# Routing one-hots and token products from 2-byte operands, the chunk index innermost

## The chip, the cores and the metric

The kernel runs on one core of one Trainium2 chip. Times are device microseconds (us) from the start to the end of one execution; the numbers compared are medians of several executions.

## What is computed

Linear attention without a softmax, followed by a mixture of experts with one expert per token.

```python
kv  = einsum('bhsd,bhse->bhde', k, v)            # b=8, h=8, s=576, d=e=64
out = einsum('bhsd,bhde->bhse', q, kv)
x   = out / sqrt(mean(out**2, -1) + 1e-6) * g_norm   # heads joined: x is [4608, 512]
logits = x @ w_gate                              # [4608, 8]
e = argmax(logits, axis=1); gate = softmax(logits)[e]
# in order of the tokens: the n-th token of an expert gets slot n, up to capacity 1152
out[i] = gate[i] * (relu(x[i] @ w1[e]) @ w2[e])  # w1: 512 x 1024, w2: 1024 x 512; zero if not kept
```

## The kernel before

**Two stages.** The first stage takes the eight images one after another: k, v and q are loaded, TensorE forms k'v (L736), transposes q (L802) and multiplies (L820); ScalarE and VectorE copy the results out of PSUM into `o_sb`; squares are summed (L846, L851). Then comes the routing of the image, `route`, mostly small VectorE instructions: reciprocal roots by Newton steps (L896 to L903), logits, the expert `mv_all`, and the token's place `pos_all` among the tokens of its expert, for which TensorE counts over the 128 partitions (L971). A token's row goes to `x_dram`. An image has 576 tokens; they lie on 128 partitions in C = 5 chunks.

Meanwhile the weights of the expert with the most tokens so far are loaded and split into two 2-byte halves (`w1h`, `w1l`, `w2h`, `w2l`: L390 or L392 for the high half, L396 for the low half, L356 and L360 for their scale), and once five images are routed the first 384 tokens of that expert are gathered (L452), normalised (L460), transposed through one PSUM bank (L470), split (L700 and L478) and multiplied with its weights (L555, L560, L563, then L601).

The second stage goes through the eight experts by rank: 640 slots and fewer each, weights loaded and split for the next expert while TensorE multiplies for this one.

**The table.** What the second stage needs is a table of the tokens: for each expert and each slot the token's number. It is built by TensorE, in `enter` (L1016), one matmul per chunk and five per image, all adding up in one PSUM bank `tab`. The stationary operand `ohl` is a one-hot of the low seven bits of a token's place, 128 columns; the moving operand `rhs` has 96 columns: 48 pairs of expert and high bits of the place, for each the token's number in a high and a low part. `rhs` is the product of the column one-hot `ohh` (48 columns) with the two parts `tok_hl`. The one-hots compare an index with a constant row: `iota128` (L210) and `cols` (L247), filled by GpSimd at the start. The three instructions are `low_hot` (L998), `col_hot` (L1003) and `tokens` (L1009). `read_table` (L1102 on) turns the table into row numbers; it runs after image 4 for the early expert and after image 7 for all, and `rank_experts` puts the experts in order after that.

**Widths.** `ohl` and `rhs` are 2 bytes wide (float16), `ohh`, `cols`, `lo`, `col`, `tok_hl` 4 bytes (float32). The five chunks are the outermost index of `ohl`, `ohh` and `rhs` behind the partition.

**The order.** Every operation of both stages is entered in a `Plan` with its engine, or a choice of engines, and a planned duration in us; the plan works out start times by taking, engine by engine, the operation that can start first and by its key among equals, and the instructions are emitted in that order. Each engine takes its own instructions in the order in which they were emitted. In the line `o2 = V(0.73, low_hot, [lo], takes=(lh,))` 0.73 us is the planned duration on VectorE, `[lo]` what it waits for, and `lh` the buffer that it takes, which has one copy (`rings`). `TOKENS` gives `tokens` a choice: VectorE for 0.57 us or GpSimd for 2.0.

Of the kernel before, what the change touches and what calls it, by code (L numbers as in the profile page):

```python
# [10 lines left out]
F16 = mybir.dt.float16  # L11
F32 = mybir.dt.float32
I32 = mybir.dt.int32
AF = mybir.ActivationFunctionType
ALU = mybir.AluOpType
# [5 lines left out]
NHI = 6  # L21
# [19 lines left out]
LAG_ELSE = 0.21  # L41
SQUARES = 'XXAAX'
TOPS = ('VVVV', 'AAAA')
TOKENS = (('V', 0.57), ('P', 2.0))
FIRST = -50.0
KEY = 10.0
EARLY_TILES = 1
# [111 lines left out]
def attention_moe_kernel(  # L159
# [12 lines left out]
    nc = tc.nc  # L172
    NB, H, S, D = q.shape
    N, DM = out.shape
    E = w_gate.shape[1]
    F = w1.shape[2]
    P = 128
    C = 5
# [6 lines left out]
    NT = NB * C  # L185
    W = E * NHI

    cst = ctx.enter_context(tc.tile_pool(name="cst", bufs=1))
# [20 lines left out]
    iota128 = cst.tile([P, P], F32, name="iota128")  # L209
# [15 lines left out]
    nc.vector.tensor_scalar(out=tok1, in0=tok_i[:, 0], scalar1=pair[:, 1:2], scalar2=None, op0=ALU.add)  # L225
    nc.vector.tensor_copy(tok_i[:, 0], tok1)

    tok_hl = cst.tile([P, 2, NT], F32, name="tok_hl")
    nc.vector.tensor_scalar(out=tok_i[:, 1], in0=tok_i[:, 0], scalar1=63, scalar2=None, op0=ALU.bitwise_and)
    nc.vector.tensor_copy(tok_hl[:, 1], tok_i[:, 1])  # L230
    nc.vector.tensor_scalar(out=tok_i[:, 1], in0=tok_i[:, 0], scalar1=6, scalar2=None, op0=ALU.logical_shift_right)
# [11 lines left out]

    slot_pos = cst.tile([P, W], F32, name="slot_pos")
    nc.gpsimd.iota(slot_pos, [[0, E], [P, NHI]], base=0, channel_multiplier=1, allow_small_or_imprecise_dtypes=True)
    cols = cst.tile([P, W], F32, name="cols")
    nc.gpsimd.iota(cols, [[-64, E], [1, NHI]], base=64 * E, channel_multiplier=0, allow_small_or_imprecise_dtypes=True)  # L247
    desc8 = cst.tile([P, E], F32, name="desc8")
    nc.vector.tensor_scalar(out=desc8, in0=iota_e, scalar1=-1.0, scalar2=float(E), op0=ALU.mult, op1=ALU.add)

# [44 lines left out]
    mv_all = cst.tile([P, NT], F32, name="mv_all")  # L295
# [382 lines left out]
    tab, misc = bank("tab"), bank("misc")  # L678
# [13 lines left out]
    op = plan.op  # L692
# [163 lines left out]
    def bc(ap, n):  # L856
        return ap.rearrange("p (c o) -> p c o", o=1).broadcast_to([P, C, n])
# [3 lines left out]
    def route(b, oh, ssh, outs, sums):  # L861

        key = (b + 1) * C - SOON
        cs = slice(b * C, (b + 1) * C)
        o_sb, ss = oh.t, ssh.t.rearrange("p c h -> p (c h)")
        z = {}
        tile_ = lambda nm, shape, dt=F32, bufs=2: z.setdefault(nm, at.tile([P] + shape, dt, name=nm, bufs=bufs))
        ne = NEWTON[b]
        eng = {"V": nc.vector, "P": nc.gpsimd}
        fast = {"V": 0.11, "P": 0.32}[ne]  # L870
        V = lambda t, f, deps, **kw: op(("V", t), lambda e: f(), deps, key, **kw)
# [15 lines left out]
        o = V(0.1, half, sums + lasts.get(b - 2, []), takes=(), uses=(ssh,))  # L887
        o = V(0.1, guess, [o])
        o = V(0.1, guess2, [o])
# [18 lines left out]
        for i in range(3):  # L908
            for j in range(4):
                o = op((ne, fast), newton(i, j), [o], key)  # L910
        rinv = o
        lth, hh, rh, lh = new("lt"), new("ohh"), new("rhs"), new("ohl")
# [21 lines left out]
        o = V(0.65, logits, [lt], uses=(lth,))  # L934
        o = V(0.11, most, [o])
# [21 lines left out]
        o = V(0.11, firsts, [dl])  # L957
        o = V(0.11, which, [o])
# [24 lines left out]
        def position():  # L983
            nc.vector.tensor_reduce(out=pos_all[:, cs], in_=z["inc"], axis=AX.X, op=ALU.max)

        o = V(0.11, mine, [bp])
        reads.append(o)
        pos = V(0.11, position, [o])
        lo_i = V(0.07, lambda: nc.vector.tensor_scalar(out=tile_("lo_i", [C], I32), in0=pos_all[:, cs], scalar1=P - 1,
                                                       scalar2=None, op0=ALU.bitwise_and), [pos])  # L990
        hi_i = V(0.07, lambda: nc.vector.tensor_scalar(out=tile_("hi_i", [C], I32), in0=pos_all[:, cs], scalar1=7,
                                                       scalar2=None, op0=ALU.logical_shift_right), [pos])
        lo = V(0.07, lambda: nc.vector.tensor_copy(tile_("lo", [C]), z["lo_i"]), [lo_i])
        col = V(0.07, lambda: nc.vector.scalar_tensor_tensor(out=tile_("col", [C]), in0=mv_all[:, cs], scalar=64.0,
                                                             in1=z["hi_i"], op0=ALU.mult, op1=ALU.add), [hi_i])

        def low_hot():
            nc.vector.tensor_tensor(out=tile_("ohl", [C, P], F16, 1),  # L998
                                    in0=iota128.rearrange("p (o w) -> p o w", o=1).broadcast_to([P, C, P]),
                                    in1=bc(z["lo"], P), op=ALU.is_equal)  # L1000

        def col_hot():
            nc.vector.tensor_tensor(out=tile_("ohh", [C, W], F32, 1),  # L1003
                                    in0=cols.rearrange("p (o w) -> p o w", o=1).broadcast_to([P, C, W]),
                                    in1=bc(z["col"], W), op=ALU.is_equal)

        def tokens(e):
            s4 = [P, C, 2, W]
            eng[e].tensor_tensor(out=tile_("rhs", [C, 2, W], F16, 1),  # L1009
                                    in0=z["ohh"].rearrange("p c (o w) -> p c o w", o=1).broadcast_to(s4),  # L1010
                                    in1=tok_hl[:, :, cs].rearrange("p i (c o) -> p c i o", o=1).broadcast_to(s4),
                                    op=ALU.mult)

        def enter(e):
            for c in range(C):
                nc.tensor.matmul(tab[:, 0:2 * W], lhsT=z["ohl"][:, c, :], rhs=z["rhs"][:, c], start=(b == 0 and c == 0),  # L1016
                                 stop=(b == NB - 1 and c == C - 1), skip_group_check=True)

        o = V(0.32, col_hot, [col], takes=(hh,))
        o = op(TOKENS, tokens, [o], key, (rh,), (hh,))  # L1020
        o2 = V(0.73, low_hot, [lo], takes=(lh,))
        ent = op(("T", 0.21), enter, [o, o2] + enters[-1:] + readers.pop("tab", []), FIRST, (), (rh, lh))
        enters.append(ent)

# [7 lines left out]
        o = V(0.11, sums_, [ex])  # L1032
        o = V(0.07, plus, [o])
# [484 lines left out]
    op = plan.op  # L1518
# [200 lines left out]
```

## Time and profile before

| what | value |
|---|---|
| median of 3 runs | 569.44 us (569.03 to 570.95) |
| profiled execution | 574.34 us, its span 572.5 us |
| TensorE matmul busy | 530.4 us, 93% of the span |
| VectorE busy | 389.3 us, 68% |
| ScalarE busy | 256.6 us, 45% |
| GpSimd busy | 204.9 us, 36% |
| mean granted TensorE clock | 0.975 of full speed |

The span reaches from the first to the last instruction of the profiled execution. Busy shares are averages over stages that have different limits; the groups of rows further down are cut by stage and by instruction. In them PE is TensorE's matmul, PEld its weight load, DVE VectorE, ACT ScalarE, POOL GpSimd, SP the engine that issues loads.

### The profile page before, as it was taken

How to read it: one execution, taken by the hardware profiler on the slowest of the kernel's cores; microseconds unless marked ns; L12 is line 12 of the kernel's file. 1: busy time of each engine (PE TensorE's matmuls, PEld its weight loads, DVE VectorE, ACT ScalarE, POOL GpSimd, SP SyncE). 2: the span in 40 equal slices, each digit the busy share in tenths (PEclk: the TensorE clock that was granted, in tenths of full speed). 3: DMA queues.
4: the chain of work that ended last, by engine and by line, in shares of the span. 5: the costliest groups of instructions: out<-in, count | busy, mean ns of one | idle time of the engine just before them, and what ended most of it. 6: DMA issues, size and time to landing. Idle time of an engine off the chain costs nothing.

```text
span 572.5 us, 11807 instructions
## 1 busy us (share of the span) xinstructions
PE 530.4 (93%) x4450; PEld 365.0 (64%) x4450; DVE 389.3 (68%) x1064; ACT 256.6 (45%) x502; POOL 204.9 (36%) x246
## 2 busy tenths in 40 slices
PE   5999896886897999999999999999999999999995
PEld 4888785774544666546754675677477558648743
DVE  4488687799977989998998677295848606203800
ACT  1687675496412662644715525263353426212211
POOL 3003334354334373345506440742453374021011
PEclk9999898697999999999999999999999999999998
DMA  8999999543249789599678755563645233010000
GB/s 279 358 354 315 370 357 374 198 148 154 94 142 363 153 214 294 138 316 163 201 183 207 177 150 155 166 170 99 200 155 128 87 103 58 6 55 21 2 37 32
DMA packets 81905, 102.71 MB, mean 179 GB/s; under 512 B 39148, under 2 KB 63724, under 8 KB 80818
## 3 DMA queue, kind: packets, MB, share of 16 engines
q1 hardware_dynamic: 74240, 70.50, 43.3%
q0 software_dynamic: 7584, 31.38, 16.2%
q8 instruction: 37, 0.61, 0.4%
q14 instruction: 26, 0.21, 0.1%
q10 hardware_dynamic: 18, 0.02, 0.0%
HBM read 73.20 MB, written 20.68 MB: 164 GB/s over the span
## 4 chain that ended last, share of the span: by engine, by line
issue 32%; PE 31%; POOL 12%; DVE 12%; DMA 9%; ACT 2%; SPq 2%; POOLq 0%; DVEq 0%
PE hp L555 10%; PE yp L601 8%; POOL out_dram L631 4%; PE op L820 4%; POOL pair L488 4%; DMA q_sb<-in_q_dram 3%; DMA xs<-pair 3%; PE a L736 3%; POOL xg L452 2%; DVE w1l L396 2%; PE op L555 2%; POOL xm L460 2%; DVE ss L851 2%; PE qp L802 2%; DMA v_sb<-in_v_dram 1%
## 5 line engine op out<-in xcount | busy, mean ns | idle before, releaser
L555 PE MATMUL hp<-xs,w1h 128*128 128x320 f16 (+6 forms) x960 | 134.2, 292 | 1.9 <-DVE hl L563 0.9
L555 PEld LDWEIGHTS <-w1h 128*128 128x128 f16 x1024 | 99.6, 98 | 38.8 <-issue 6.3
L631 POOL DMA_INDIRECT out_dram<-ysb,si x42 | 42.7, 1016 | 161.3 <-ACT ysb L626 152.0
L601 PEld LDWEIGHTS <-hh 128*128 128x128 f16 x560 | 54.2, 98 | 63.2 <-issue 1.1
L560 ACT ACTIVATE hh<-hp 128x320 f16<-128x320 f32 (+7 forms) x64 | 41.0, 640 | 106.6 <-PE hp L555 101.9
L356 DVE TENSOR_REDUCE am<-raw 128x1 f32<-128x512 f32 x120 | 75.9, 674 | 6.6 <-DMA raw<-in_moe_w_dram 6.6
L626 ACT ACTIVATE ysb<-yp,ysc 128x512 f32<-128x512 f32 (+5 forms) x41 | 28.1, 685 | 99.9 <-PE yp L601 90.7
L555 PE MATMUL hp<-xs,w1l 128*128 128x320 f16 (+6 forms) x480 | 72.0, 292 | 0.0
L563 DVE SCALAR_TENSOR_TENSOR hl<-hp,hh 128x320 f16<-128x320 f32 (+7 forms) x64 | 47.4, 740 | 32.9 <-ACT hh L560 31.4
L601 PE MATMUL yp<-w2h,hh 128*128 128x512 f16 x272 | 65.3, 379 | 0.8 <-ACT ysb L626 0.8
L601 PE MATMUL yp<-w2l,hh 128*128 128x512 f16 x272 | 64.5, 379 | 0.0
L601 PE MATMUL yp<-w2h,hl 128*128 128x512 f16 x272 | 64.4, 379 | 0.0
L820 PE MATMUL op<-kv_bd,qt 128*128 128x144 f32 x320 | 55.6, 311 | 5.7 <-ACT o_sb L700 2.9
L555 PEld LDWEIGHTS <-w1l 128*128 128x128 f16 x512 | 49.9, 98 | 16.4
L452 POOL DMA_INDIRECT xg<-x_dram,gi x42 | 44.7, 1064 | 30.8 <-DVE gt L465 10.7
L616 DVE COPY yt<-yp 128x256 f32<-128x256 f32 (+4 forms) x7 | 2.9, 415 | 75.9 <-PE yp L610 66.3
L396 DVE SCALAR_TENSOR_TENSOR w2l<-raw,sw,w2h 128x512 f16<-128x512 f32 x64 | 50.1, 826 | 4.1 <-ACT w2h L390 4.1
L820 PEld LDWEIGHTS op<-kv_bd,qt 128*128 128x128 f32 x320 | 46.1, 203 | 9.5 <-ACT o_sb L700 5.0
L396 DVE SCALAR_TENSOR_TENSOR w1l<-raw,sg,w1h 128x512 f16<-128x512 f32 x64 | 50.6, 823 | 1.5 <-ACT w1h L390 1.5
L488 POOL TENSOR_TENSOR pair<-xm,pair 128x512 f16<-128x512 f32 (+5 forms) x26 | 33.7, 1295 | 49.7 <-ACT pair L484 49.6
L601 PEld LDWEIGHTS <-hl 128*128 128x128 f16 x280 | 27.2, 98 | 31.8
L460 POOL TENSOR_TENSOR xm<-xg 128x512 f32<-128x512 f32 (+5 forms) x34 | 39.8, 1170 | 16.2 <-DVE pair L488 11.1
(249 smaller groups left out, 708.5 us busy)
## 6 DMA issues: line engine op xcount, KB each, us to landing
raw<-in_moe_w_dram SPq DMA_DIRECT2D x64, 512.0 KB, 5.2
x_dram<-o_sb POOLq DMA_DIRECT2D x8, 720.0 KB
k_sb<-in_k_dram SPq DMA_DIRECT2D x16, 320.0 KB, 6.1
v_sb<-in_v_dram SPq DMA_DIRECT2D x16, 320.0 KB, 6.5
q_sb<-in_q_dram SPq DMA_DIRECT2D x16, 320.0 KB, 6.6
x_dram<-o_sb POOLq DMA_DIRECT2D x8, 576.0 KB
k_sb<-in_k_dram SPq DMA_DIRECT2D x16, 256.0 KB, 3.4
v_sb<-in_v_dram SPq DMA_DIRECT2D x16, 256.0 KB
```

The source lines that it names most:

```text
L356: nc.vector.tensor_reduce(out=am()[:, p:p + 1], in_=raw[:, sl(p)], axis=AX.X, op=ALU.max, apply_absolute_value=True)
L396: nc.vector.scalar_tensor_tensor(out=wl[:, sl(p)], in0=raw[:, sl(p)], scalar=z["s"], in1=wh[:, sl(p)], op0=ALU.mult, op1=ALU.subtract)
L452: nc.gpsimd.indirect_dma_start(out=self.xg[i][0:n], out_offset=None, in_=x_dram[0:self.rows, :], in_offset=bass.IndirectOffsetOnAxis(ap=se ...
L460: eng.tensor_tensor(out=self.xm[i][0:n].rearrange("p (h d) -> p h d", h=H), in0=xg[:, :, 0:D], in1=xg[:, :, D:D + 1].broadcast_to([n, H, D ...
L488: eng.tensor_tensor(out=pair[0:n, 1], in0=self.xm[i][0:n], in1=pair[0:n, 0], op=ALU.subtract)
L555: nc.tensor.matmul(self.view(hp)[:, v], lhsT=w[:, c, f * P:(f + 1) * P], rhs=x[:, c, u * hw:(u + 1) * hw], start=(t == 0 and c == 0), stop ...
L560: nc.scalar.activation(self.out(self.hh, j), self.view(hp), AF.Relu)
L563: nc.vector.scalar_tensor_tensor(out=self.out(self.hl, j), in0=self.view(hp), scalar=0.0, in1=self.out(self.hh, j), op0=ALU.max, op1=ALU.s ...
L601: nc.tensor.matmul(yp[0:n, 0:DM], lhsT=h[:, j, o:o + n], rhs=w[:, j, :], start=(m == 0), stop=(m == len(self.terms) - 1))
L626: nc.scalar.activation(self.ysb[0:n], yp[0:n, 0:DM], AF.Copy, scale=self.ysc[0:n, i:i + 1])
L631: nc.gpsimd.indirect_dma_start(out=(disjoint.pop() if disjoint else out)[:, :], out_offset=bass.IndirectOffsetOnAxis(ap=self.sidx[0:n, col ...
L820: nc.tensor.matmul(ph.t[:, p * 2 * XW:(p + 1) * 2 * XW], lhsT=qt.t[:, (2 * w + p) * P:(2 * w + p + 1) * P], rhs=x, start=True, stop=True)
```

## The change

The constants and the small index tensors become 2 bytes wide, `cols` is repeated for each chunk, a constant `lows` of 128 x 5 takes the place of `iota128` in the low one-hot, and the chunk index becomes the innermost one of `ohl`, `ohh` and `rhs`. In the two comparisons and in the product every operand then walks in steps of one element along the five chunks, and the matmul reads both its operands with a step of five elements (10 bytes). The planned durations are changed, and the token product loses its choice of GpSimd.

```diff
-TOKENS = (('V', 0.57), ('P', 2.0))
+TOKENS = ('V', 0.31)
...
-    tok_hl = cst.tile([P, 2, NT], F32, name="tok_hl")
+    tok_hl = cst.tile([P, 2, NT], F16, name="tok_hl")
...
-    cols = cst.tile([P, W], F32, name="cols")
-    nc.gpsimd.iota(cols, [[-64, E], [1, NHI]], base=64 * E, ...)
+    cols = cst.tile([P, W, C], F16, name="cols")
+    nc.gpsimd.iota(cols, [[-64, E], [1, NHI], [0, C]], base=64 * E, ...)
+    lows = cst.tile([P, P, C], F16, name="lows")
+    nc.gpsimd.iota(lows, [[1, P], [0, C]], base=0, ...)
...
-        lo = V(0.07, lambda: nc.vector.tensor_copy(tile_("lo", [C]), z["lo_i"]), [lo_i])
-        col = V(0.07, lambda: nc.vector.scalar_tensor_tensor(out=tile_("col", [C]), ...
+        lo = V(0.07, lambda: nc.vector.tensor_copy(tile_("lo", [C], F16), z["lo_i"]), [lo_i])
+        col = V(0.07, lambda: nc.vector.scalar_tensor_tensor(out=tile_("col", [C], F16), ...
...
         def low_hot():
-            nc.vector.tensor_tensor(out=tile_("ohl", [C, P], F16, 1),
-                                    in0=iota128.rearrange("p (o w) -> p o w", o=1).broadcast_to([P, C, P]),
-                                    in1=bc(z["lo"], P), op=ALU.is_equal)
+            nc.vector.tensor_tensor(out=tile_("ohl", [P, C], F16, 1), in0=lows,
+                                    in1=z["lo"].rearrange("p (o c) -> p o c", o=1).broadcast_to([P, P, C]), op=ALU.is_equal)
         def col_hot():
-            nc.vector.tensor_tensor(out=tile_("ohh", [C, W], F32, 1),
-                                    in0=cols.rearrange("p (o w) -> p o w", o=1).broadcast_to([P, C, W]),
-                                    in1=bc(z["col"], W), op=ALU.is_equal)
+            nc.vector.tensor_tensor(out=tile_("ohh", [W, C], F16, 1), in0=cols,
+                                    in1=z["col"].rearrange("p (o c) -> p o c", o=1).broadcast_to([P, W, C]), op=ALU.is_equal)
         def tokens(e):
-            s4 = [P, C, 2, W]
-            eng[e].tensor_tensor(out=tile_("rhs", [C, 2, W], F16, 1),
-                                    in0=z["ohh"].rearrange("p c (o w) -> p c o w", o=1).broadcast_to(s4),
-                                    in1=tok_hl[:, :, cs].rearrange("p i (c o) -> p c i o", o=1).broadcast_to(s4),
-                                    op=ALU.mult)
+            s4 = [P, 2, W, C]
+            eng[e].tensor_tensor(out=tile_("rhs", [2, W, C], F16, 1),
+                                 in0=z["ohh"].rearrange("p (o w) c -> p o w c", o=1).broadcast_to(s4),
+                                 in1=tok_hl[:, :, cs].rearrange("p i (o c) -> p i o c", o=1).broadcast_to(s4), op=ALU.mult)
         def enter(e):
             for c in range(C):
-                nc.tensor.matmul(tab[:, 0:2 * W], lhsT=z["ohl"][:, c, :], rhs=z["rhs"][:, c], ...
+                nc.tensor.matmul(tab[:, 0:2 * W], lhsT=z["ohl"][:, :, c], rhs=z["rhs"][:, :, :, c], ...
...
-        o = V(0.32, col_hot, [col], takes=(hh,))
+        o = V(0.18, col_hot, [col], takes=(hh,))
         o = op(TOKENS, tokens, [o], key, (rh,), (hh,))
-        o2 = V(0.73, low_hot, [lo], takes=(lh,))
+        o2 = V(0.4, low_hot, [lo], takes=(lh,))
```

## Rows read from the trace of the kernel before

**Rows 1.** Windows of 10 us: busy us (instructions), TensorE clock, DMA share, GB/s.
```profile
core 0: us, PE busy (x) PEld busy (x) DVE busy (x) ACT busy (x) POOL busy (x), PEclk, DMA share, GB/s
30.00:40.00 10.00, 9.62 (x129) 8.91 (x127) 9.33 (x40) 7.61 (x21) 0.00 (x0) 1.00 1.08 356
110.00:120.00 10.00, 9.55 (x74) 8.58 (x75) 8.94 (x26) 8.10 (x23) 9.05 (x7) 0.79 0.26 69
120.00:130.00 10.00, 6.52 (x48) 5.56 (x46) 9.94 (x22) 7.68 (x20) 3.12 (x3) 1.00 0.54 178
130.00:140.00 10.00, 5.82 (x37) 4.84 (x38) 9.88 (x38) 8.79 (x25) 6.79 (x15) 0.73 0.48 187
140.00:150.00 10.00, 9.27 (x60) 5.27 (x59) 9.05 (x42) 5.14 (x10) 4.33 (x4) 0.92 0.33 132
170.00:180.00 10.00, 7.57 (x41) 4.00 (x40) 5.31 (x20) 2.79 (x5) 4.40 (x5) 1.00 0.93 306
190.00:200.00 10.00, 10.00 (x60) 5.68 (x59) 9.80 (x29) 7.82 (x15) 4.57 (x5) 1.00 0.80 136
```

**Rows 2.** Groups of VectorE instructions, 28 to 180 us: busy us, mean ns | idle before.
```profile
L998 DVE TENSOR_TENSOR ohl<-iota,lo 128x640 f16<-128x640 f32 x8 | 6.7, 834 | 0.0
L1009 DVE TENSOR_TENSOR rhs<-ohh,tok_hl 128x480 f16<-128x480 f32 x7 | 4.5, 649 | 0.1
L702 DVE COPY kv_bd<-kvs 64x256 f32<-64x256 f32 x12 | 3.6, 300 | 2.9 <-ACT kvs L700 2.7
L1003 DVE TENSOR_TENSOR ohh<-cols,col 128x240 f32<-128x240 f32 x8 | 3.3, 414 | 0.0
L702 DVE COPY kvt<-a 128x256 f32<-128x256 f32 x2 | 0.8, 422 | 0.5 <-PE a L760 0.5
```

**Rows 3.** Time line, image 4: start us, us [idle before <-releaser].
```profile
107.50 0.64 DVE L1009 TENSOR_TENSOR rhs<-ohh,tok_hl 128x480 f16<-128x480 f32 x1
109.39 0.72 ACT L390 ACTIVATE w1h<-raw,sg 128x512 f16<-128x512 f32 x1 [5.18 <-DVE sg L385]
```

**Rows 4.** Time line, image 5, up to the first product of the early expert.
```profile
136.46 0.65 DVE L1009 TENSOR_TENSOR rhs<-ohh,tok_hl 128x480 f16<-128x480 f32 x1
...
137.03 0.68 DVE L478 TENSOR_TENSOR xs<-x,xs 128x512 f16<-128x512 f32 x1
...
137.85 0.88 PE L470 MATMUL x<-ident,xm 128*128 128x128 f32 x4 [0.32 <-DVE xs L478]
...
138.81 0.58 ACT L700 CAST xs<-x 128x512 f16<-128x512 f32 x1
...
139.44 1.44 PE L555 MATMUL op<-xs,w1h 128*128 128x384 f16 x4 [0.70 <-ACT xs L700]
```

**Rows 5.** Time line, image 6.
```profile
150.51 0.54 DVE L563 SCALAR_TENSOR_TENSOR hl<-op,hh 128x384 f16<-128x384 f32 x1
...
151.10 0.81 PE L555 MATMUL op<-xs,w1h 128*128 128x384 f16 x4 [0.88 <-DVE hl L563]
```

**Rows 6.** Time line, image 7, and the end of the chain behind it.
```profile
162.85 0.66 DVE L1009 TENSOR_TENSOR rhs<-ohh,tok_hl 128x480 f16<-128x480 f32 x1
...
163.70 0.38 PE L1016 MATMUL tab<-rhs,ohl 128*128 128x96 f16 x5
...
179.26 0.46 PE L470 MATMUL xp<-ident,xm 64*128 64x64 f32 x4 [2.16 <-DVE xm L460]
```

**Rows 7.** Instructions on `ohl`: ns min/median/max, first and last start us.
```profile
L1016 PEld LDWEIGHTS <-ohl x40: 95/98/151, 43.7 to 163.8; 128*128 128x128 f16 x40
L1016 PE MATMUL tab<-rhs,ohl x40: 203/206/288, 44.4 to 163.9; 128*128 128x96 f16 x40
L998 DVE TENSOR_TENSOR ohl<-iota,lo x8: 807/824/908, 42.0 to 161.7; 128x640 f16<-128x640 f32 x8
```

**Rows 8.** Line 283, the transposes of the gate weights, in the same columns.
```profile
L283 PEld LDWEIGHTS misc<-ident,wrow x8: 180/198/198, 3.8 to 4.6; 4*128 4x128 f32 x8
```

**Rows 9.** The page's costliest groups: busy us, mean ns of one.
```profile
L820 PEld LDWEIGHTS op<-kv_bd,qt 128*128 128x128 f32 x320 | 46.1, 203 | 9.5 <-ACT o_sb L700 5.0
```

**Rows 10.** Time line of the start: GpSimd's fills and the first use.
```profile
3.11 0.32 POOL L247 IOTA cols<- 128x48 f32 x1
3.32 2.10 POOL L681 MEMSET kv_bd<- 128x1152 f32 x2
...
13.87 0.82 ACT L700 COPY kv_bd<-kvs 64x256 f32<-64x256 f32 x2
```

More of the change, by code (lines that the diff above doesn't have):

```diff
@@ L245, in attention_moe_kernel @@
     nc.gpsimd.iota(slot_pos, [[0, E], [P, NHI]], base=0, channel_multiplier=1, allow_small_or_imprecise_dtypes=True)
-    cols = cst.tile([P, W], F32, name="cols")
-    nc.gpsimd.iota(cols, [[-64, E], [1, NHI]], base=64 * E, channel_multiplier=0, allow_small_or_imprecise_dtypes=True)
+    cols = cst.tile([P, W, C], F16, name="cols")
+    nc.gpsimd.iota(cols, [[-64, E], [1, NHI], [0, C]], base=64 * E, channel_multiplier=0, allow_small_or_imprecise_dtypes=True)
+    lows = cst.tile([P, P, C], F16, name="lows")
+    nc.gpsimd.iota(lows, [[1, P], [0, C]], base=0, channel_multiplier=0, allow_small_or_imprecise_dtypes=True)
     desc8 = cst.tile([P, E], F32, name="desc8")
@@ L992, in route @@
                                                        scalar2=None, op0=ALU.logical_shift_right), [pos])
-        lo = V(0.07, lambda: nc.vector.tensor_copy(tile_("lo", [C]), z["lo_i"]), [lo_i])
-        col = V(0.07, lambda: nc.vector.scalar_tensor_tensor(out=tile_("col", [C]), in0=mv_all[:, cs], scalar=64.0,
+        lo = V(0.07, lambda: nc.vector.tensor_copy(tile_("lo", [C], F16), z["lo_i"]), [lo_i])
+        col = V(0.07, lambda: nc.vector.scalar_tensor_tensor(out=tile_("col", [C], F16), in0=mv_all[:, cs], scalar=64.0,
@@ L1014, in enter @@
         def enter(e):
             for c in range(C):
-                nc.tensor.matmul(tab[:, 0:2 * W], lhsT=z["ohl"][:, c, :], rhs=z["rhs"][:, c], start=(b == 0 and c == 0),
+                nc.tensor.matmul(tab[:, 0:2 * W], lhsT=z["ohl"][:, :, c], rhs=z["rhs"][:, :, :, c], start=(b == 0 and c == 0),
                                  stop=(b == NB - 1 and c == C - 1), skip_group_check=True)
-        o = V(0.32, col_hot, [col], takes=(hh,))
+        o = V(0.18, col_hot, [col], takes=(hh,))
         o = op(TOKENS, tokens, [o], key, (rh,), (hh,))
-        o2 = V(0.73, low_hot, [lo], takes=(lh,))
+        o2 = V(0.4, low_hot, [lo], takes=(lh,))
```

## The prediction

> **What bounds the kernel now.** I read the windows first, to cut the span into stages, then the groups of VectorE instructions between 28 and 180 us, then the time lines around each place where the edited instructions run. The windows show three stages [rows 1]. Up to about 110 us the DMA share is at 1.0 and the loads set the pace: VectorE is 93% busy at 30 to 40 us, but so is TensorE, and the transfers cannot come sooner. From 110 to about 140 us the DMA share falls to 0.26 to 0.54, TensorE is down to 6.5 and 5.8 busy us of 10, and VectorE stands at 8.9 to 9.9 of 10: here the order of VectorE's queue sets the pace. From 140 to 180 us TensorE is mostly busy with the early expert but still loses 0.7 us in one window and 2.4 in another. From 190 us TensorE has 10.0 of 10, with VectorE close behind at 9.8; whatever is gained must be gained before that, and it comes through only if VectorE's work for the next expert is moved ahead along with TensorE's.
>
> **The three VectorE instructions.** Each image has one low one-hot (640 elements per partition), one column one-hot (240) and one token product (480). They take 834, 414 and 649 ns [rows 2], 1897 ns in all; one of the eight token products runs on GpSimd. From the first two, (834 - 414) / 400 elements is 1.05 ns an element, over 162 ns that do not depend on the length. The change makes all operands 2 bytes wide and puts the chunks innermost, so that every operand walks in steps of one element, in runs of five. No row shows a two-input VectorE instruction of that kind and of any length, so I bound it. At one end the element cost stays: nothing is saved. At the other it halves: 162 + 336, 162 + 126 and 162 + 244 ns, that is 498, 288 and 406, together 1192 ns and 0.71 us less per image. The nearest row for a halving is a copy of 256 4-byte elements inside SBUF, 300 ns against 422 ns for a copy of the same length out of PSUM [rows 2]: less 162 ns it is 0.54 against 1.02 ns an element, so this engine does halve its element cost where operands allow. I take the halving, and keep zero for the range.
>
> The runs are of five, an odd number. If two elements could not be paired across the end of a run, five elements would take three steps in place of five, the saving would be four fifths (0.57 us per image), and the sum below 1.8 us in place of 2.2.
>
> [...]
>
> **Where that saving is on the path.** Eight images times 0.71 is 5.7 us of VectorE time, but the eight low one-hots start between 42.0 and 161.7 us [rows 7], and five of them before 110 us. Image by image:
>
> Images 0 to 3: nothing, the loads hide them (the first window of [rows 1]); without that cover they would be worth 2.8 us.
>
> Image 4, at 106 to 108 us: the scale of the first expert weights stands behind its token product, and ScalarE starts splitting them at 109.39, having idled 5.18 us for that scale [rows 3]. But the last queries are still landing and TensorE is 9.55 busy in the next window, so I count half: 0.35 us.
>
> Image 5, at 135 to 137 us: the clearest place. Behind the token product of 136.46 stands the low half of the second group of gathered rows (137.03); that frees the one PSUM bank for the third transpose (137.85), whose cast (138.81) lets TensorE begin the early expert at 139.44 [rows 4]. All 0.71 us pass.
>
> Image 6, at 149 to 151 us: the low half of a hidden tile at 150.51 stands behind both one-hots, and TensorE idles 0.88 us for it [rows 5]. The two one-hots shrink by 0.46 us, and the wait with them.
>
> Image 7, at 161.7 us on: token product, table, slots and gathered rows follow one another, and TensorE idles 2.16 us at the end of that chain for the last group of rows [rows 6]. 0.71 us pass; the ranking of the experts and with it the loads of the next weights hang on the same VectorE queue, so they move ahead too.
>
> Sum: 0.35 + 0.71 + 0.46 + 0.71 = 2.2 us.
>
> **What is added.** The table matmul now reads both operands with a step of 10 bytes. The rows to hold against it are 98 ns for a contiguous 2-byte weight load and 206 ns for its matmul [rows 7], and 198 ns for a 4-byte load from four partitions with a step of 32 bytes [rows 8], no more than the 203 ns that the contiguous 4-byte loads take in the same trace [rows 9]. A strided stationary operand is not dearer there, so I take zero; the upper bound is that a load doubles to the 4-byte price, five times 105 ns, and that a 96-column matmul, five in 0.38 us [rows 6], doubles too: about 0.9 us per image, of which images 6 and 7 would feel 1.8 us and the others little.
>
> [...]
>
> GpSimd fills two larger constants at the start, 240 and 640 elements in place of 48. The 48 took 0.32 us [rows 10], 6.7 ns an element, so 880 elements take at most 5.9 us and the fill of the two zeroed matrices ends at about 11 us instead of 5.4. They are first written at 13.87 us, and GpSimd has nothing else to do before the first output writes: zero, hidden by 2.8 us even at that price. The token product that ran on GpSimd costs VectorE 0.4 us in an image that the loads hide. The casts that feed the new operands keep their length and only change the output type.
>
> **The order.** The emission order is worked out from planned durations, and those fall by 0.73 us per image. All later choices (ScalarE or VectorE, VectorE or GpSimd, which ready operation first) may fall differently, in both stages. The trace cannot price this; the waits of TensorE between 100 and 200 us are each at most 2.2 us [rows 6], and one or two such waits more or fewer is what I allow.
>
> **Rivals.** (a) The forecast, 2.2 us: chance 0.52. (b) The saving is absorbed. For it: between 140 and 180 us TensorE is itself busy for most of the time, and behind a shorter VectorE queue it may wait for gathered rows or loads instead. Against it: image 5's chain has no other late arrival. It also holds the case that the instructions do not speed up at all, or that the strided operands eat the gain. 0 to 1.2 us off, 569 us; chance 0.26. (c) Slower, through the new order: at 110 to 165 us, where VectorE has no room [rows 1], a low half that TensorE needs is queued behind a later image's routing, or the reverse. One such wait of 2.2 us cancels the gain (569.4), two make it 571.6; from 3.9 us of new waits on the kernel is slower by over 0.3%. Chance 0.16. (d) The new order happens to close some of the 7.7 us that TensorE idles from 120 to 140 us [rows 1]: 2 to 3 us more, 564.5; chance 0.06.
>
> **The numbers.** The profiled execution took 574.34 us, its span 572.5; the sum gives 572.1 for it. The median of the runs is 569.44, 4.9 us below that execution; I take the same 2.2 us off: 567.2. Its own range is 565.6 to 568.6: all four images in full (2.84) and a little from the order, to 0.8 left over. The range for 8 in 10 reaches to most of (c) and stops short of (d): 565.2 to 571.2. About 0.3%, 1.7 us, is what the runs can tell from no change. Faster by more than that: 0.42 of (a), 0.06 of (d): 0.48. Slower: 0.13 of (c). Within: the rest, 0.39.
>
> **What would show it.** The three groups at about 0.50, 0.29 and 0.41 us, all eight token products on VectorE; the 40 weight loads of the table still at 98 ns; TensorE's first 384-column matmul near 138.4 us and the last table matmul near 162 us; the end of the idle stretches about 2 us sooner, and the 10.0 busy windows unchanged behind them. If the groups keep 0.8, 0.4 and 0.65, the step on element cost is wrong; if they fall but the first 384-column matmul does not move, the path is; if TensorE shows new waits after 190 us, the order took it.

## The result and the profile after

The changed kernel is slower by 1.4%: 579.31 us, the median of 4 runs (577.7 to 580.7), against 570.2 us for the kernel before, run beside it (4 runs, 569.03 to 573.39); the ratio, from all of these runs, is 1.0143, with a 95% interval of 1.011 to 1.0175 (the two medians alone give 1.016). The prediction was 567.2 us, with a range that ended at 571.2. The profiled execution took 580.7 us, its span is 578.9; busy are TensorE 534.6 us (92%), VectorE 393.1 (68%), ScalarE 253.9 (44%) and GpSimd 208.4 (36%). VectorE's busy time is not shorter than before (389.3 us): part of what the three instructions save comes back at the start, where two of its instructions last 4.47 and 4.31 us (last section).

The three instructions and the table matmul after the change, in the columns of [rows 7]:

```profile
L1015 PEld LDWEIGHTS <-ohl x40: 117/118/152, 42.6 to 163.5; 128*128 128x128 f16 x40
L1015 PE MATMUL tab<-rhs,ohl x40: 268/288/294, 43.6 to 163.6; 128*128 128x96 f16 x40
L1000 DVE TENSOR_TENSOR ohl<-lows,lo x8: 544/550/580, 41.8 to 161.7; 128x640 f16<-128x640 f16 x8
L1004 DVE TENSOR_TENSOR ohh<-cols,col x8: 294/302/355, 42.3 to 162.2; 128x240 f16<-128x240 f16 x8
L1009 DVE TENSOR_TENSOR rhs<-ohh,tok_hl x8: 442/450/485, 43.1 to 162.5; 128x480 f16<-128x480 f16 x8
```

So the instructions did become shorter: medians of 550, 302 and 450 ns where [rows 2] have means of 834, 414 and 649 (their medians are 824, 402 and 648). The strided matmul became dearer: 118 ns against 98 for the load and 288 against 206 for the matmul [rows 7]. Neither can make 9 us: eight images save 8 x 0.57 us and pay 8 x 0.33 us for the table matmul (five in 0.71 us where [rows 6] have 0.38).

Windows of 10 us in the columns of [rows 1], first of the kernel before, with its longest wait of TensorE in them, then of the changed one:

```profile
70.00:80.00 10.00, 9.51 (x124) 9.01 (x124) 8.41 (x32) 7.16 (x19) 5.04 (x14) 1.00 1.03 371
80.00:90.00 10.00, 9.55 (x144) 8.69 (x143) 9.41 (x35) 7.59 (x20) 3.53 (x10) 1.00 0.98 332
90.00:100.00 10.00, 4.64 (x30) 4.19 (x29) 7.31 (x21) 4.92 (x14) 2.72 (x8) 0.86 1.06 392
100.00:110.00 10.00, 8.14 (x96) 7.19 (x97) 7.17 (x27) 3.41 (x8) 0.54 (x1) 0.67 0.82 288
```

```profile
98.02 1.09 PE L802 MATMUL qp<-ident,q_sb 128*128 128x128 f32 x4 [5.13 <-DMA q_sb<-in_q_dram]
```

```profile
70.00:80.00 10.00, 6.78 (x78) 6.38 (x73) 4.12 (x16) 3.15 (x9) 3.18 (x12) 0.83 1.02 402
80.00:90.00 10.00, 7.33 (x93) 6.71 (x93) 9.87 (x35) 6.22 (x17) 1.59 (x4) 1.00 1.08 399
90.00:100.00 10.00, 8.91 (x78) 7.64 (x78) 7.20 (x22) 4.55 (x11) 3.19 (x12) 0.66 0.69 260
100.00:110.00 10.00, 6.31 (x72) 5.69 (x71) 9.74 (x30) 7.53 (x17) 7.43 (x6) 1.00 0.51 192
120.00:130.00 10.00, 7.35 (x55) 6.42 (x55) 9.94 (x27) 8.45 (x25) 3.85 (x3) 1.00 0.64 212
130.00:140.00 10.00, 6.30 (x48) 4.76 (x49) 10.00 (x36) 7.11 (x21) 7.56 (x17) 0.90 0.32 133
170.00:180.00 10.00, 5.98 (x32) 3.04 (x31) 5.07 (x19) 2.09 (x4) 4.89 (x6) 0.95 0.90 309
```

TensorE (the first busy column) is short of work from 70 to 90 and again from 100 to 110 us, where before it has its gap from 90 to 100, a wait of 5.13 us for loaded queries. VectorE (the third) has 4.12 us of work in one window and is full in the next. From 120 to 140 us VectorE is full as it was in [rows 1]. The time line of the fourth image (image 3) and behind, in the changed kernel:

```profile
75.30 0.63 PE L804 MATMUL qp<-ident,q_sb 128*128 128x128 f32 x4 [2.91 <-DMA q_sb<-in_q_dram]
...
85.38 0.68 DVE L358 TENSOR_REDUCE am<-raw 128x1 f32<-128x512 f32 x1
...
87.45 0.67 DVE L358 TENSOR_REDUCE am<-raw 128x1 f32<-128x512 f32 x1
...
88.97 0.30 DVE L1004 TENSOR_TENSOR ohh<-cols,col 128x240 f16<-128x240 f16 x1
...
89.28 0.67 DVE L358 TENSOR_REDUCE am<-raw 128x1 f32<-128x512 f32 x1
89.88 0.48 DVE L1009 TENSOR_TENSOR rhs<-ohh,tok_hl 128x480 f16<-128x480 f16 x1
...
90.41 0.71 PE L1015 MATMUL tab<-rhs,ohl 128*128 128x96 f16 x5 [3.08 <-DVE rhs L1009]
...
109.07 0.70 PE L1015 MATMUL tab<-rhs,ohl 128*128 128x96 f16 x5 [2.72 <-DVE rhs L1009]
...
137.67 1.22 PE L557 MATMUL op<-xs,w1h 128*128 128x384 f16 x4 [1.85 <-DVE xs L704]
...
179.77 0.68 PE L472 MATMUL xp<-ident,xm 64*128 64x64 f32 x4 [3.48 <-DVE xm L462]
180.92 3.36 PE L557 MATMUL hp<-xs,w1h 128*128 128x320 f16 x12 [0.46 <-ACT xs L702]
```

The wait at 75.30 is for loaded queries, as before but earlier. Line 358 finds the largest absolute values of the early expert's weights, eight instructions of 0.67 us; their result is wanted only at 96 us. Three of them now stand ahead of the fourth image's token product (89.88), and TensorE's queue has the table matmul at its head: TensorE waits 3.08 us for it, and the transposes and products behind it wait too. At 109.07 TensorE waits again, 2.72 us, for the fifth image's token product. In the profile of before no wait of over 0.4 us for a token product stands ahead of 137 us.

One profile of an order tells little of the place of a loss. The profiled execution of before has its first 384-column matmul at 139.44 us [rows 4], later than the changed kernel; three experiments below with that order have it at 129.47, 134.40 and 134.60. The experiments are therefore judged by their ratios first, and the marks are read with that scatter in mind.

### The profile page after: what moved, and what is told of

The parts are those of the page before. It is cut to its first block, busy times and chain, and to the rows that moved or that the text cites. A ratio compares the mean times of both kernels' runs of the same rounds, so it can differ in the third digit from the quotient of the medians.

```text
span 578.9 us, 11807 instructions
## 1 busy us (share of the span) xinstructions
PE 534.6 (92%) x4450; PEld 365.4 (63%) x4450; DVE 393.1 (68%) x1068; ACT 253.9 (44%) x496; POOL 208.4 (36%) x249
## 4 chain that ended last, share of the span: by engine, by line
PE 44%; issue 25%; DVE 13%; POOL 9%; DMA 6%; ACT 1%; SPq 0%; POOLq 0%; DVEq 0%
PE hp L557 15%; PE yp L603 14%; PE op L822 4%; POOL out_dram L633 3%; PE a L738 3%; POOL pair L490 2%; PE yp L612 2%; DVE w1l L398 2%; DVE ss L853 2%; POOL xg L454 2%; PE op L557 2%; DMA k_sb<-in_k_dram 2%; PE qp L804 2%; DMA q_sb<-in_q_dram 2%; POOL xm L462 1%
## 5 line engine op out<-in xcount | busy, mean ns | idle before, releaser
L557 PE MATMUL hp<-xs,w1h 128*128 128x320 f16 (+6 forms) x960 | 137.6, 296 | 1.8 <-DVE hl L565 1.4
L557 PEld LDWEIGHTS <-w1h 128*128 128x128 f16 x1024 | 101.2, 100 | 40.9 <-issue 4.3
L490 POOL TENSOR_TENSOR pair<-xm,pair 128x512 f16<-128x512 f32 (+5 forms) x29 | 37.1, 1281 | 64.3 <-ACT pair L486 64.0
L398 DVE SCALAR_TENSOR_TENSOR w1l<-raw,sg,w1h 128x512 f16<-128x512 f32 x64 | 52.0, 846 | 1.7 <-ACT w1h L392 1.7
L392 ACT ACTIVATE w2h<-raw,sw 128x512 f16<-128x512 f32 x62 | 40.3, 712 | 10.1 <-PE yp L612 7.5
```

The costliest lines, as they stand in the source:

```text
L392: nc.scalar.activation(wh[:, sl(p)], raw[:, sl(p)], AF.Copy, scale=z["s"])
L398: nc.vector.scalar_tensor_tensor(out=wl[:, sl(p)], in0=raw[:, sl(p)], scalar=z["s"], in1=wh[:, sl(p)], op0=ALU.mult, op1=ALU.subtract)
L490: eng.tensor_tensor(out=pair[0:n, 1], in0=self.xm[i][0:n], in1=pair[0:n, 0], op=ALU.subtract)
L557: nc.tensor.matmul(self.view(hp)[:, v], lhsT=w[:, c, f * P:(f + 1) * P], rhs=x[:, c, u * hw:(u + 1) * hw], start=(t == 0 and c == 0), stop ...
```

## The experiments

Ratios are to the kernel before, run on the same chip, with the 95% interval. Two marks from the profiled execution of each kernel go with them: the start of the first 384-column matmul, and of the last table matmul (137.67 and 163.6 us in the changed kernel).

**Instructions or order.** The emission order follows from the planned durations, so the two parts of the change can be taken apart. The first kernel has the new instructions and the old durations, and with them the old order on every engine; the second the reverse.

```diff
-TOKENS = ('V', 0.31)
+TOKENS = (('V', 0.57), ('P', 2.0))
...
-        o = V(0.18, col_hot, [col], takes=(hh,))
+        o = V(0.32, col_hot, [col], takes=(hh,))
...
-        o2 = V(0.4, low_hot, [lo], takes=(lh,))
+        o2 = V(0.73, low_hot, [lo], takes=(lh,))
```

> The changed instructions and operands with the planned durations of before (0.32, 0.73, and the old choice for the token product), so that every engine's order is that of before. If the order lost the time: TensorE reaches the first products of the rank-0 expert about 2 us sooner than before, 567 to 569 us, 0.2 to 0.5% faster. If the operands lost it (strided reads by TensorE, GpSimd's longer fills at the start): 575 us and more.

> The instructions of before with the planned durations of the change, so that the order is that of the changed kernel. If the order lost the time: 577 to 582 us, with the idle stretch of TensorE at about 176 to 180 us and a half clock behind it. If the operands lost it: 569 to 572 us.

New instructions in the old order: 567.34 us, 0.9969 [0.9937, 1.0001], the marks at 129.5 and 154.7. Old instructions in the new order: 578.39 us, 1.0159 [1.0125, 1.0194], the marks at 137.6 and 164.5, with TensorE waiting 3.66 and 3.27 us for the token products of the fourth and fifth image. The whole loss goes with the order: with either set of instructions the new order costs 1.6 to 1.7% against the old one.

**The fills.** GpSimd's larger constants make the start later, so in two kernels VectorE copies them from small ones, once in the new order and once in the old.

```diff
-    nc.gpsimd.iota(lows, [[1, P], [0, C]], base=0, ...
+    nc.vector.tensor_copy(lows, iota128.rearrange("p (w o) -> p w o", o=1).broadcast_to([P, P, C]))
...
+    nc.vector.tensor_copy(cols, cols1.rearrange("p (w o) -> p w o", o=1).broadcast_to([P, W, C]))
```

> The changed kernel, but VectorE copies the two large constants from small ones, so that GpSimd's start is that of before. TensorE's first products of k and v come 2 to 3 us sooner than in the changed kernel. If the late start is carried to the end: 576 to 577 us. If the loads and the order hide it: 578 to 581 us.

> Both: the order of before, and VectorE fills the constants. If the order lost the time: 566 to 568.5 us, at or a little under the run with the old order alone. If the operands lost it: still 573 us and more, less only by what the late start costs.

577.99 us, 1.0135 [1.01, 1.017], in the new order and 569.1 us, 0.9985 [0.996, 1.001], in the old. TensorE's first product comes at 8.4 and 8.1 us in place of 10.4: the late start, shown in the last section, costs nothing that can be measured.

**Which stage.** Each stage has its own plan, so one can be planned with the new and the other with the old durations; the instructions are the new ones in both kernels.

```diff
+        o.alt = [("V", 0.32)]
...
     plan.emit()
+    for o in plan.ops:
+        o.todo, o.next, o.end = 0, [], None
+        o.ways = getattr(o, "alt", o.ways)
+    plan.free = dict(FREE)
+    plan.place()
```

> The changed instructions; the first stage is emitted in the order of the changed kernel, the second in that of before (the plan of the first stage is timed once more with the old durations before the second is planned). If the first stage's order lost the time: 575 to 579 us, the last table matmul at about 164 us. If the second's: 567 to 570 us.

> The changed instructions; the first stage in the order of before, the second in that of the changed kernel. If the second stage's order lost the time: 575 to 579 us, with the last table matmul at 155 to 160 us. If the first's: 567 to 570 us.

New order in the first stage alone: 573.67 us, 1.0077 [1.0047, 1.0107], the marks at 135.5 and 162.0; that lies between the two times expected. In the second alone: 567.68 us, 0.997 [0.9943, 0.9996], at 131.2 and 156.8. The first stage is needed for the loss and makes about half of it by itself; with the new second stage behind it the loss is larger by 0.7%, though the second stage's order costs nothing behind the old first stage.

**Neighbouring orders.** Is it that the durations are too short? The trace of after has 0.22, 0.37 and 0.47 us from start to start of these instructions. Five kernels change nothing but the three numbers, here for `col_hot`, `tokens` and `low_hot`:

```diff
-0.18, 0.31, 0.40
+0.22, 0.37, 0.47
+0.19, 0.32, 0.41
+0.17, 0.30, 0.39
+0.20, 0.33, 0.42
+0.16, 0.29, 0.38
```

and a sixth takes 0.01 us from each of the old numbers in the kernel before:

```diff
-0.32, 0.57, 0.73
+0.31, 0.56, 0.72
```

> The changed kernel with planned durations as its trace shows them from start to start, 0.22, 0.37 and 0.47 us in place of 0.18, 0.31 and 0.40. If planned durations that are too short lost the time: back to 567 to 570 us. If any new order is as likely to be bad: anywhere between 568 and 582, and not near 568 for that reason.

> The kernel before with the three planned durations 0.01 us lower, its instructions untouched; the order changes in many places all the same. If the kernel is not sensitive to the order as such: 569 to 571 us, no difference. If it is: a difference of more than 0.3%, and rather slower.

> The changed kernel with its three planned durations 0.01 us longer (0.32, 0.19, 0.41). If the loss is a matter of durations that are too short (measured: 0.45, 0.30 and 0.55 us long), 0.01 us changes little: 576 to 580 us. If it is one chance order among many, this order is another draw, and lies anywhere from 566 to 580 us.

> The changed kernel with its three planned durations 0.01 us shorter (0.30, 0.17, 0.39). Too short durations as the cause: 577 to 581 us, no better than the changed kernel. A chance order among many: anywhere from 566 to 580 us.

> The changed kernel with its three planned durations 0.02 us longer (0.33, 0.20, 0.42): one more order. If orders near that of the changed kernel scatter, with its own at the slow end: 566 to 573 us. If the shortness of the durations were the cause: 577 us or more.

> The changed kernel with its three planned durations 0.02 us shorter (0.29, 0.16, 0.38): one more order. Scatter: 566 to 573 us. Shortness as the cause: 577 us or more.

Measured durations: 567.14 us, 0.9971 [0.9943, 0.9999]. The kernel before, 0.01 shorter: 568.04, 0.9978 [0.9952, 1.0003]. After with 0.01 longer: 571.08, 1.0019 [0.9993, 1.0045]; 0.01 shorter: 568.34, 0.9972 [0.994, 1.0004]; 0.02 longer: 570.23, 1.0007 [0.9979, 1.0035]; 0.02 shorter: 566.67, 0.992 [0.9889, 0.9951]. Numbers still shorter than the change's lose nothing either, so the loss does not come from numbers that are too short. One hundredth of a microsecond in the three planned durations moves the time by up to 1.7%, about 10 us; the order of the change is the worst of these six (its own and the five around it).

**The waiting matmul moved.** On TensorE alone, the table matmuls of an image are put behind the work that was planned to start up to 3 us after them; all else is the changed kernel.

```diff
+HOLDS = (3.0, 3.0, 3.0, 3.0, 3.0, 3.0, 3.0, 0)
...
+            while n < len(t) and t[n] not in after and t[n].start <= h.start + h.hold:
+                n += 1
+            t.insert(n, h)
...
+        ent.hold = HOLDS[b]
```

> Every instruction and every engine's order of the changed kernel; on TensorE alone the five table matmuls of an image are moved behind the products, k'v sums and transposes that were planned to start up to 3 us after them (for the fourth image behind eight transposes-and-products, for the fifth behind some 3.5 us of such work). If the loss comes from TensorE standing at the table matmul until VectorE has the token product (3.08 us at 90.4 and 2.72 us at 109.1 in the changed kernel), these two waits shrink below 1 us each, the first 384-column matmul comes 4 to 6 us before 137.7, and the time is 571 to 574 us. If those waits only show what VectorE's order delays anyway, other waits of the same length take their place and the time stays at 577 to 580 us.

583.19 us, 1.0227 [1.0183, 1.0271]: slower still, and slower than either time expected. My theory, that TensorE loses the time because the matmul stands too early in its queue, fell. The time line of TensorE in this kernel shows where the time went:

```profile
89.16 0.71 PE L1039 MATMUL tab<-rhs,ohl 128*128 128x96 f16 x5 [0.54 <-DVE rhs L1033]
...
92.52 0.27 PE L395 MATMUL misc<-ident,a 128*1 128x128 f32 x1 [1.92 <-DVE a L392]
...
108.87 2.29 PE L846 MATMUL op<-kv_bd,qt 128*128 128x144 f32 x8 [3.09 <-ACT qt L726]
...
137.14 4.02 PE L581 MATMUL op<-xs,w1h 128*128 128x384 f16 x12 [1.51 <-DVE xs L728]
```

The wait of 3.08 us is down to 0.54, but 1.92 us stand in its place at 92.52, now for VectorE's result from the weight maxima, and 3.09 us at 108.87, for ScalarE's copy of the transposed queries. The orders of VectorE, ScalarE and GpSimd are as they were; TensorE meets other late results in place of the one that it no longer waits for.

**The work ahead of the token product moved.** So the edit belongs on VectorE. In this kernel three instructions are moved and nothing else: the three maxima that stand between the fourth image's routing steps come behind its token product.

```diff
+            for o in tops:
+                o.hold = 7.0 if i == 0 else 0
...
+        t = rows["V"]
```

> Every instruction and every engine's order of the changed kernel, but on VectorE the three maxima of the early weights (0.67 us each) that stand between the routing steps of the fourth image come behind its token product, in front of the other five maxima. If the time is lost because VectorE's queue puts work with time to spare ahead of the token product that TensorE waits for, TensorE's wait of 3.08 us at 90.4 shrinks to about 1.1 us, everything behind it moves up by 2 us, and the time is 576.5 to 578 us. If, as when the table matmul was moved, another wait takes its place, the time stays at 579 us or above.

574.05 us against 568.66 for the kernel before, 1.0096 [1.0064, 1.0128]. Against 1.0143 [1.011, 1.0175] a third of the loss is gone, more than expected; but the two intervals overlap, and the difference of 0.47% is hardly larger than its own uncertainty. The time line:

```profile
88.56 0.46 DVE L1032 TENSOR_TENSOR rhs<-ohh,tok_hl 128x480 f16<-128x480 f16 x1
88.94 4.83 DVE L381 TENSOR_REDUCE am<-raw 128x1 f32<-128x512 f32 x8
89.08 0.71 PE L1038 MATMUL tab<-rhs,ohl 128*128 128x96 f16 x5 [1.44 <-DVE rhs L1032]
...
106.85 0.71 PE L1038 MATMUL tab<-rhs,ohl 128*128 128x96 f16 x5 [2.77 <-DVE rhs L1032]
...
134.43 1.45 PE L580 MATMUL op<-xs,w1h 128*128 128x384 f16 x4 [1.85 <-DVE xs L727]
```

The wait falls from 3.08 to 1.44 us, the first 384-column matmul comes at 134.43 in place of 137.67, the last table matmul at 160.4 in place of 163.6 (both within the scatter of a single order). The wait for the fifth image's token product is still there, 2.77 us.

**Which images.** Short durations for some images alone, the old ones for the others:

```diff
+        old = b >= 4
+        o = V(0.32 if old else 0.18, col_hot, [col], takes=(hh,))
+        o = op(TOKENS if old else ('V', 0.31), tokens, [o], key, (rh,), (hh,))
+        o2 = V(0.73 if old else 0.4, low_hot, [lo], takes=(lh,))
```

with `b < 4` and `b not in (2, 3)` in the two others.

> Instructions of the changed kernel; its short planned durations for the images 0 to 3 alone, the longer ones of the kernel before for the images 4 to 7. If the loss starts in the order of the images whose loads set the pace, it stays: 577 to 580 us, with the first 384-column matmul at about 137.5. If it starts in the order of the images behind the loads, the time falls to 567 to 570 us and that matmul comes at about 130.

> The counterpart: short planned durations for the images 4 to 7 alone, the longer ones for the images 0 to 3. If the loss starts in the first four images: 566 to 569 us. If it starts in the last four: 576 to 580 us.

> Instructions of the changed kernel; its short planned durations for the images 2 and 3 alone, the longer ones of the kernel before for all others. If the loss that short durations for the images 0 to 3 bring (575.4 us) starts at the third or fourth image, behind which the waits at 75 and 90 us stand: 573 to 578 us. If it starts at the first two images: 565 to 569 us.

Images 0 to 3: 575.42 us, 1.0089 [1.0062, 1.0116]. Images 4 to 7: 565.49 us, 0.9927 [0.989, 0.9964], with the order of 0.02 us shorter the fastest measured here, and faster than both kernels. Images 2 and 3: 568.24, 0.9992 [0.9961, 1.0024]. A loss comes with the first four, but not as expected: its marks are 130.6 and 156.5, as early as in the old order, although the three maxima stand ahead of the fourth image's token product there too and TensorE waits 3.09 us for it. So this kernel's profiled execution lost its time behind the first stage. By its expectation the third kernel puts the start of the loss at images 0 and 1; these two alone were not run.

**The layout alone.** All operands 2 bytes wide, the old order, but the chunks outermost as before: the comparisons and the product then read their second operand with a step of zero, and the matmul reads both of its operands without a gap. The edit is shown against the changed kernel.

```diff
-            nc.vector.tensor_tensor(out=tile_("ohl", [P, C], F16, 1), in0=lows,
+            nc.vector.tensor_tensor(out=tile_("ohl", [C, P], F16, 1),
+                                    in0=lows.rearrange("p (o w) -> p o w", o=1).broadcast_to([P, C, P]),
...
-                nc.tensor.matmul(tab[:, 0:2 * W], lhsT=z["ohl"][:, :, c], rhs=z["rhs"][:, :, :, c], ...
+                nc.tensor.matmul(tab[:, 0:2 * W], lhsT=z["ohl"][:, c, :], rhs=z["rhs"][:, c], ...
```

> The order of the kernel before and 2-byte operands throughout, but with the chunk index outermost as before, so that the chunk's own value is read with a step of zero and the matmul reads both operands contiguously. If the shorter instructions come from the step of one along the chunks, the three instructions go back to about 0.82, 0.41 and 0.65 us, and the time is that of the kernel before, 569 to 570 us. If the 2-byte width alone brings it, they take 0.55, 0.30 and 0.45 us as in the changed kernel, the table matmul keeps 206 ns and 98 ns, and the time is 566 to 567 us, at or below that of the same order with the chunks innermost.

```profile
L1017 PEld LDWEIGHTS <-ohl x40: 95/98/99, 43.9 to 160.0; 128*128 128x128 f16 x40
L1017 PE MATMUL tab<-rhs,ohl x40: 203/206/217, 44.6 to 160.0; 128*128 128x96 f16 x40
L1000 DVE TENSOR_TENSOR ohl<-lows,lo x8: 812/822/909, 42.2 to 157.8; 128x640 f16<-128x640 f16 x8
L1005 DVE TENSOR_TENSOR ohh<-cols,col x8: 396/402/469, 43.0 to 158.6; 128x240 f16<-128x240 f16 x8
L1011 DVE TENSOR_TENSOR rhs<-ohh,tok_hl x7: 637/649/659, 43.9 to 159.0; 128x480 f16<-128x480 f16 x7
```

570.81 us, 1.0013 [0.9978, 1.0047], and the old durations to within some 10 ns of [rows 2]: the width alone gave nothing here, with 1.05 ns an element, (822 - 402) / 400, as before. The instructions gained only with the chunks innermost (550, 302 and 450 ns in after), and that layout is also what the matmul pays for: 118 and 288 ns in after, 98 and 206 here.

## Why the prediction was wrong

**The step that failed is "The order".** It said that later choices may fall differently, that the trace cannot price this, and allowed one or two waits of TensorE of at most 2.2 us. The runs price it: with the instructions of before, the new order alone costs 1.59%, about 9 us, and with the new instructions the old order costs nothing. Rival (c), with 0.16, had the right sign, but it was sized too small and put in another place. It placed the harm at 110 to 165 us, a low half behind a later image's routing. By the runs the loss comes with the planned durations of images 0 to 3 (1.0089, against 0.9927 for images 4 to 7), that is, in the stage that the step on images 0 to 3 had given up as hidden by the loads. The loads may hide a shorter instruction there; they do not hide another order.

**Which wait carries the loss is not shown.** The candidate is the token product of the fourth image behind the weight maxima. The maxima that stand ahead of it on VectorE, by the time lines, and the ratios:

| maxima ahead | kernels | ratios |
|---|---|---|
| none | old order with new instructions; with VectorE's fill; with the new second stage; old nudged; 0.01 and 0.02 shorter; last four images; third and fourth image; chunks outermost | 0.9969, 0.9985, 0.997, 0.9978, 0.9972, 0.992, 0.9927, 0.9992, 1.0013: mean 0.997 |
| three or four | after; old instructions; with VectorE's fill; with the old second stage; table matmul moved; first four images | 1.0143, 1.0159, 1.0135, 1.0077, 1.0227, 1.0089: mean 1.014 |
| three or four | measured durations; 0.01 and 0.02 longer | 0.9971, 1.0019, 1.0007: mean 1.000 |

The six kernels of the second line all have the changed kernel's planned durations for images 0 to 3, so they are not independent draws, and something else in those orders can be the cause. The three of the third line have orders of their own, with the same maxima ahead of the same product, and lose nothing that can be measured. Their waits for it are 3.49, 3.10 and 3.29 us; with durations 0.01 us longer even the second wait is there, and the first 384-column matmul is no earlier than in the changed kernel:

```profile
90.01 0.71 PE L1015 MATMUL tab<-rhs,ohl 128*128 128x96 f16 x5 [3.10 <-DVE rhs L1009]
...
108.40 0.71 PE L1015 MATMUL tab<-rhs,ohl 128*128 128x96 f16 x5 [2.84 <-DVE rhs L1009]
...
138.26 3.25 PE L557 MATMUL op<-xs,w1h 128*128 128x384 f16 x12 [0.67 <-ACT xs L702]
```

So the two waits do not by themselves make a kernel slower. Moving the three maxima gave back 0.47% of the 1.43%, at the edge of what the runs can tell; that they cost time in this order is likely, not shown.

**Where the time goes** is seen no better than to halves, by the marks of all profiled executions in the one order or the other:

| order | kernel | first 384-column matmul | last table matmul | from there to the end |
|---|---|---|---|---|
| old | before | 139.4 | 163.9 | 408.6 |
| old | new instructions | 129.5 | 154.7 | 410.0 |
| old | with VectorE's fill | 134.6 | 159.6 | 406.4 |
| old | chunks outermost | 134.4 | 160.0 | 410.3 |
| new | after | 137.7 | 163.6 | 415.3 |
| new | old instructions | 137.6 | 164.5 | 410.1 |
| new | with VectorE's fill | 137.6 | 164.0 | 411.9 |

The means differ by 3.1 us at the first mark, by 4.5 at the second and by 3.6 in the stretch behind it. With the old order the first mark alone scatters by 10 us. The forecast had named a first 384-column matmul near 138.4 us as a sign that it holds. 137.67 was measured, and the kernel is slower all the same: a mark that scatters so much cannot decide it.

**What stays open** is therefore most of the mechanism. The wait for the fifth image's token product was not removed by itself. And one part lies behind the first stage: from the last table matmul to the end of the span there are 415.3 us in after, 414.3 with the table matmul moved and 415.6 with the first four images, against 406.4 to 411.9 in all the other kernels. The same three, and they alone, have TensorE idle for 2.0 to 2.3 us in seven gaps at the turned products of 64 columns, for nothing that the profile shows (0.8 us at most in the others); in after:

```profile
210.07 0.27 PE L612 MATMUL yp<-hh,w2h 128*128 128x64 f16 x3 [0.37 <-issue]
...
212.47 0.28 PE L612 MATMUL yp<-hh,w2h 128*128 128x64 f16 x4 [0.46 <-issue]
```

Each kernel has one profiled execution, so whether the gaps go with the order or come and go was not tried. The kernel with VectorE's fill has the order of after, has none, and is as slow.

**TensorE's clock goes with the loss.** The mean granted clock is known for every run. The median over a kernel's runs is 0.969 to 0.978 in the seven kernels above 1.002, and 0.979 to 0.989 in all others; the kernel before has 0.979 to 0.980 beside them. In after the granted clock is 0.50 of full speed for 6.8 us from 178.9 on, and 1.00 from 174 up to there; it falls towards the end of the wait of 3.48 us shown above, and the product behind it runs at that clock, 3.36 us where twelve matmuls of this shape took 1.90 us in before (at 180.18, clock 1.00):

```profile
178.90:185.70 6.80, 5.47 (x23) 3.23 (x24) 4.86 (x12) 0.69 (x2) 0.96 (x1) 0.50 1.03 403
```

Over the 116 runs of the kernel before, compared within each chip, a mean clock lower by 0.01 goes with 3.4 us more. By that, as an estimate, the lower clock stands for one to three of the 8 to 9 us in the three kernels with the new order; whether it is a cause beside the waits or only follows from them was not tried.

**The three instructions.** The element cost fell from 1.05 ns to (550 - 302) / 400, which is 0.62 ns, not to the half that I took. The saving is 0.57 us per image by the medians, in place of 0.71: what the prediction gave for five elements in three steps. That was an estimate, and no run shows the steps: whether unpaired ends or something else in the runs of 10 bytes makes the difference, no run tells.

**The strided matmul** was taken at zero. It costs 0.33 us per image, a third of the upper bound of 0.9. With the step of 10 bytes the load is 1.2 times as long (118 ns against 98), the matmul 1.4 times (288 against 206). The row of 4-byte weights that I went by, [rows 8], was the wrong neighbour; why this step costs time was not shown.

**The sum** with measured sizes: 0.29 + 0.57 + 0.38 + 0.57 for images 4 to 7, less 0.33 each for the table matmuls of images 6 and 7, is 1.15 us in place of 2.2. The runs have the instructions by themselves three times: in the old order against before, 0.31% or 1.8 us; against the chunks outermost, 1.0013 - 0.9969, 2.5 us; in the order of after, 1.0159 - 1.0143, 0.9 us. Each of the three has an interval of 0.3% or more to either side and none is clear of zero by itself; their mean is 1.7 us. The step was right in kind, its size by the measured lengths is half of what I took, and the runs contradict neither figure. It was the smaller effect.

**GpSimd's fills** were taken at zero and cost zero, though by another way than the one argued: two of VectorE's instructions end just behind them, at 8.69 us (last section), TensorE's first product comes at 10.4 us, where before it came at 7.8, and that time does not reach the end. New waits of TensorE after 190 us were to be the sign of a harmful order; about half of the loss was there ahead of the last table matmul at 164 us.

## What to carry to other kernels

Where instructions are emitted by a plan, a changed duration is two changes, a shorter instruction and another order, and the second can be several times the first: 0.01 us in a plan moved this kernel by up to 10 us, while three instructions a third shorter are worth one or two. Measure them apart, with the new instructions in the old order first, and then draw several orders: two of those tried here (0.992 and 0.9927) beat both kernels with the very instructions of the slower one. A long wait in a trace is not yet the cause: here a kernel with the same two waits lost nothing. Moving the instruction that waits made this kernel slower; moving what stood ahead of the late result, on the engine that makes it, gave something back, at the edge of the noise.

## What the runs showed of the hardware

Two small VectorE instructions lasted until GpSimd's work beside them was over, 4.47 and 4.31 us, where the same two take 1.00 and 0.85 us in the kernel before (to 5.46 us), whose fills end at 5.42 [rows 10]. At the start of after, in the columns of [rows 10]:

```profile
3.10 1.05 POOL L247 IOTA cols<- 128x240 f16 x1
...
4.11 2.54 POOL L249 IOTA lows<- 128x640 f16 x1
4.22 4.47 DVE L225 TENSOR_SCALAR tok<-tok_i,pair_f 128x40 f32<-128x40 int32 x1
4.38 4.31 DVE L256 TENSOR_SCALAR even<-pair_f 128x1 f32<-128x1 f32 x1
...
6.59 2.05 POOL L683 MEMSET kv_bd<- 128x1152 f32 x2
...
10.40 3.90 PE L738 MATMUL a<-v_sb,k_sb 128*64 128x64 f32 x68
```

The two VectorE instructions, of 40 elements and of one, end at 8.69, just behind GpSimd's last fill (6.59 + 2.05 = 8.64), and TensorE's first product comes behind what follows them. In the kernel with VectorE's fill the first of them starts behind GpSimd's fills and takes 0.24 us:

```profile
6.35 0.24 DVE L225 TENSOR_SCALAR tok<-tok_i,pair_f 128x40 f32<-128x40 int32 x1
```

The two constants themselves are cheap: 4.4 ns an element for 240 and 4.0 for 640, against the 6.7 that the prediction took from the 48 of [rows 10]. A small VectorE instruction that lasts long beside GpSimd's work is seen in the first stage too, at the routing of the fifth image:

```profile
103.80 5.08 POOL L394 TENSOR_SCALAR w1h<-raw,sg 128x512 f16<-128x512 f32 x3
...
104.36 1.91 DVE L993 TENSOR_SCALAR hi_i<-pos_all 128x5 int32<-128x5 int32 x1
```

Five elements take 1.91 us while GpSimd works, where the fourth image's took 0.16 (88.11 us). In the kernel before the fifth image's took 0.16 as well (105.18 us), and GpSimd's splits came behind it, at 109.47: it is the new order that puts them side by side, ahead of the fifth image's token product, for which TensorE waits at 109.07. The kernel with durations 0.01 us longer has the same 1.91 us and loses nothing.
